# Zero fills of an attention and gated-product kernel: 64-KB pieces read from DRAM, and transfers of 3 MB

## The chip, the cores and the metric

The kernel runs on one core of one Trainium2 chip. The metric is device time in microseconds of one execution, lower is better. Times are given as the median of several runs; the profile is of one execution.

## What is computed

The program computes one decoding step of a transformer block and the gradients of everything in it. The block has an adaptive layer norm, attention over the last 4,096 positions of a cache, and a gated product:

```python
mod = (_silu(c) @ w_mod).reshape(c.shape[0], 6, 1, -1)
...
h = _layernorm(x, axis=-1) * (1 + ca) + sa
x = x + ga * _A_ref(h, A_k_cache, A_v_cache, A_wq, A_wo)
h = _layernorm(x, axis=-1) * (1 + cb) + sb
x = x + gb * _B_ref(h, B_w_gate, B_w_up, B_w_down)
return x
...
W = min(4096, max(256, Sk // 4))
k = jnp.repeat(k_cache[:, :, Sk - W:, :], rep, axis=1)
...
h = _sigmoid(g) * u
return jnp.einsum('bsf,fd->bsd', h, w_down)
```

There is one token (1,024 values), 32 query heads in 4 groups, head size 128, and a cache of 65,536 positions. The outputs are the result and its gradients for x, both caches, wq, wo, w_gate, w_up, w_down, c and w_mod, in bf16. The gradients of the two caches (out_2 and out_3) have the shape of the whole cache, and only the last 4,096 of 65,536 positions of a group are used. The other 61,440 rows of each of the 8 groups are zero and still must be written: 15.7 MB a group, 125.8 MB in all, two thirds of what the kernel writes. These writes are the zero fills.

## The kernel before

The work is written in one order by hand (the program is not rescheduled), and each engine's instructions run in that order. DMA transfers are issued on two queues. POOL issues most of them, the zero fills among them. SP issues the loads of w_down and the stores of its gradient, and some stores at the very end.

The stages, with the times of the profile: loads of keys, values and wq with the first products (to some 70 us); a first long product stage, keys times weighted values, at L646 to L679 (73 to 155 us); a second long product stage, the function `bch` at L702 (155 to about 285 us); a stretch that forms the combined weights (to some 310 us); the gated product at L1047 to L1092, seven rounds over blocks of 512 columns (to some 476 us); and a closing stage that writes the remaining gradients.

The zero fills are cut into 120 units of about 1 MB (P x ZW bf16 values, ZW = 4096) in the list `zleft` (L142 to L149). Of these, 15 units are columns of group 0 of out_2, and each of the other seven groups gives 15 contiguous units. Seven units of group 0 are "narrow" (at the places in NARROW, L38): they leave out 8 of 128 rows, which are written elsewhere.

The function `zero(n, after, big)` at L164 takes the next n units off the list and issues them on POOL. `after` makes the issue wait for a matmul, which paces the fills. A fill is written in one of three ways:

- from the tile `zeros` in SBUF, 128 rows of 8 KB (L186). The tile holds FP8 zeros, and the transfer widens them to FP32, so that it reads a quarter of what it writes;
- with `big`, from DRAM to DRAM, declared as 32 rows of 32 KB (L180). It reads zeros from `zero_src`, a unit that was filled first, again as FP8;
- narrow, also from SBUF (L173 and L176).

`big` is given in the two long product stages alone (L660 and L714). How many units are taken at each place stands in the lists Z_GA to Z_END (L48 to L57): four before the attention scores are done (L495), four at L543, 31 in the first long stage (Z_N, one at about each fourth step), 42 in the second (Z_B) with four more beside it, 5 in the stretch after it (Z_FOLD), 27 in the gated product (Z_FFN) and 3 in the closing stage.

In a round of the gated product, w_down comes in two halves of 512 KB on SP (`load_wd`, L872). PE multiplies with a half (L999), DVE forms its sums (L227) and overwrites it in place with its gradient (L223), and SP stores it (`store_wd`, L875); the next round's half is loaded into the same place when that store has landed. The blocks of w_up and w_gate are loaded by POOL (L886), used by PE (L981), overwritten by DVE and ACT, and stored by POOL (L890), in two buffers that alternate between rounds.

Of the kernel before, what the change touches and what calls it, by code (L numbers as in the profile page):

```python
# [10 lines left out]
P = 128  # L11
FP32 = mybir.dt.float32
BF16 = mybir.dt.bfloat16
FP8 = mybir.dt.float8e4
# [11 lines left out]
G = 4  # L26
# [11 lines left out]
NARROW = (15, 45, 75, 93, 103, 113, 119)  # L38

def spread(total, n):
    return [(i + 1) * total // n - i * total // n for i in range(n)]

NBP = 8
NT = 8
NGA = 9
# [5 lines left out]
Z_N = spread(31, 128)  # L53
Z_B = [n + (i in (31, 38)) for i, n in enumerate(spread(29, 43))] + [1, 1, 1, 1, 0] + [1, 0, 0, 1, 1, 1, 0, 0] + [1, 0, 1, 0, 1, 0, 0, 0]
# [4 lines left out]
def kernel(  # L59
# [26 lines left out]
    nc = tc.nc  # L86
    SKW = A_k_cache.shape[2] - W
# [16 lines left out]
    def vt(shape, name, dt=FP32):  # L104
        return pool.tile(shape, dt, name=name)
# [4 lines left out]
    ZW = 4096  # L110
    zeros = vt([P, ZW // 2], "zeros", FP8)
# [11 lines left out]
    def fill_rows(og, g):  # L123
        return og[0, g, 0:SKW, :].rearrange("r d -> (r d)")

    first_rows = fill_rows(out_2, 0).rearrange("(p x) -> p x", p=P)
    NZR = first_rows.shape[1] // ZW
    zregions = [first_rows[:, i * ZW:(i + 1) * ZW] for i in range(NZR)]
    flat = []
    for og in (out_2, out_3):  # L130
        for g in range(G):
            if og is not out_2 or g:
                whole = fill_rows(og, g).rearrange("(i x) -> i x", i=NZR)
                flat.extend(whole[i:i + 1, :] for i in range(NZR))

    zero_src = flat.pop(0)
    BIGP = 32

    def as_rows(piece, n):
        return piece.rearrange("i (p x) -> (i p) x", p=n)  # L140

    wide = [as_rows(zero_src, P)] + zregions[len(NARROW):] + flat  # L142
    narrow = zregions[0:len(NARROW)]
    zleft = []
    while narrow or wide:
        if narrow and (len(zleft) in NARROW or not wide):
            zleft.append((narrow.pop(0), True))
        else:
            zleft.append((wide.pop(0), False))  # L149
    nlen = len(NARROW)  # L150
    ncount = list(range(1, nlen + 1))
    NS = SKIP + 1
    rest = out_2[0, 0, 0:SKW, :].rearrange("r d -> (r d)").rearrange("(p x) -> p x", p=P)[0:8, 0:nlen * ZW].bitcast(FP32)
    assert nlen * 2 <= 20

    keep = [0]

    def dep(later, earlier):
        tc.add_manual_dep(later.ins, earlier.ins.name,
# [1 line left out]
                          reason="pace")  # L161

    def zero(n, after=None, big=False):  # L164
        for _ in range(n):
            if len(zleft) <= keep[0]:
                return
            region, narrow_ = zleft.pop(0)
            first = None
            if narrow_:  # L170
                nc.gpsimd.inc_swdge_sem([], [], mode="reset_dge_cursor")
                n = nlen - ncount.pop()
                first = nc.gpsimd.dma_start(  # L173
                    out=rest[0:NS, 0:nlen * 128].rearrange("p (t x) -> p t x", t=2)[:, :, n * 64:(n + 1) * 64],
                    in_=zeros[0:NS, 0:64].rearrange("p (t x) -> p t x", t=1).broadcast_to([NS, 2, 64]))
                ins = nc.gpsimd.dma_start(  # L176
                    out=region[8:P, :].bitcast(FP32).rearrange("(t p) x -> p t x", t=2),
                    in_=zeros[0:60, :].rearrange("p (t x) -> p t x", t=1).broadcast_to([60, 2, ZW // 2]))
            elif big and region.shape[0] == 1:
                ins = nc.gpsimd.dma_start(  # L180
                    out=as_rows(region, BIGP).bitcast(FP32),
                    in_=zero_src[:, 0:P * ZW // 4].rearrange("i (p x) -> (i p) x", p=BIGP).bitcast(FP8))
            else:
                if region.shape[0] == 1:
                    region = as_rows(region, P)
                ins = nc.gpsimd.dma_start(out=region.bitcast(FP32), in_=zeros[:, :])  # L186
            if after is not None:
                dep(first or ins, after)

# [19 lines left out]
    def tt(out, a, b, op):  # L209
        return nc.vector.tensor_tensor(out=out, in0=a, in1=b, op=op)  # L210
# [215 lines left out]
    for j in range(KD):  # L426
        for k in range(16):
            mm = nc.tensor.matmul(mod_ps[:, k:k + 1], lhsT=wm01_t[j][:, k * P:(k + 1) * P],
                                  rhs=cs_bf[:, j:j + 1], start=(j == 0 and k == 0), stop=(j == KD - 1),
                                  skip_group_check=True)  # L430
# [53 lines left out]
    for j in range(KD):  # L484
# [6 lines left out]
        for h in range(HQ):  # L491
            mm = nc.tensor.matmul(q_ps[:, h:h + 1], lhsT=wq_t[j][:, h * P:(h + 1) * P],  # L492
                                  rhs=h1_bf[:, j:j + 1], start=(j == 0 and h == 0), stop=(j == KD - 1),
                                  skip_group_check=True)
# [9 lines left out]
    for ch in range(8):  # L504
        ps = new_ps("sc_ps")
        for g in range(G):
            mm = nc.tensor.matmul(ps[32 * g:32 * g + 32, 0:512], lhsT=q_col2[:, HG * g:HG * g + 32],
                                  rhs=k_T[:, g, ch * 512:(ch + 1) * 512], start=True, stop=True,
                                  tile_position=(0, 32 * g))
# [132 lines left out]
    def recent(mm, lag):  # L642
        last_mm.append(mm)
        return last_mm[-lag] if len(last_mm) >= lag else last_mm[0]

    for g in range(G):  # L646
        nbank = bank_pair("n_ps", g)
        for t_ in range(KT):
            s = g * KT + t_
            vp = vp_t[(s // 2) % 2]  # L650
            if t_ % 2 == 0:
                tt(vp.rearrange("p t h d -> p (t h d)"),
                   v_nat[:, g, t_ * DH:(t_ + 2) * DH].rearrange("p (t o d) -> p t o d", t=2, o=1).broadcast_to([P, 2, HG, DH]),
                   pT2[:, g, HG * t_:HG * t_ + 2 * HG, :].rearrange("p n (o k) -> p n o k", o=1).broadcast_to([P, 2 * HG, 64, 2]),
                   ALU.mult)
            for k in range(2):
                mm = nc.tensor.matmul(nbank[k][:, :], lhsT=k_nat[:, g, t_ * DH:(t_ + 1) * DH],  # L657
                                      rhs=vp[:, t_ % 2, 4 * k:4 * k + 4, :].rearrange("p h d -> p (h d)"),
                                      start=(t_ == 0), stop=False)
            zero(Z_N[s], recent(mm, 6), True)  # L660
            if t_ == 20:
                build_bd(g)
            if s == 2:
                ok_cols(ok4)
            elif s == 4:
                ok_rows()
            elif s == 24:
                mod_gb((6, 7))
                load_wo(0)
            elif t_ % 2 == 1:  # L670
                side()
        for k in range(2):
            nc.tensor.matmul(nbank[k][:, :], lhsT=nkb_rows[:, :], rhs=bd[:, 4 * k:4 * k + 4, :].rearrange("p h d -> p (h d)"),
                             start=False, stop=True)
            c0 = (HG * g + 4 * k) * P
            nc.scalar.activation(out=N_sb[:, c0:c0 + 512], in_=nbank[k][:, :], func=ACT.Copy, scale=float(SCALE))
        load_wo(4 + g)
        if g < 3:
            jobs.extend(t_unit(h, "AA") for h in range(HG * g, HG * g + HG))  # L679
# [5 lines left out]
    bq = []  # L685
# [13 lines left out]
    nbq = len(bq)  # L699
    bbank = {}  # L700

    def bch(n=1):  # L702
        for _ in range(n):
            if not bq:
                return
            p, i, u = bq.pop(0)
            if i == 0:
                bbank[p] = bank_pair("b_ps", p)
            for a in range(4):
                h = 4 * u + a  # L710
                for k in range(2):
                    mm = nc.tensor.matmul(bbank[p][k][:, :], lhsT=a4[:, p, h, :], rhs=wo_t[u][:, a, k * 512:(k + 1) * 512],  # L712
                                          start=(i == 0 and a == 0), stop=(i == 7 and a == 3))
            zero(Z_B[nbq - 1 - len(bq)], recent(mm, 3), True)  # L714
            if i == 7:
                for k in range(2):
                    o = B_t[p][:, k * 512:(k + 1) * 512]
                    if k == 0 or p == NBP - 1:
                        nc.scalar.copy(out=o, in_=bbank[p][k][:, :])
                    else:  # L720
                        cp(o, bbank[p][k][:, :])
# [418 lines left out]
    dh1_ps = new_acc("dh1_ps")  # L1140
    for p in range(NBP):
        for it in range(KD):
# [95 lines left out]
    dh1 = vt([P, KD], "dh1")  # L1238
    cp(dh1[:, 0:NBP], dh1_ps[:, 0:NBP])
    dwo(4)  # L1240
# [34 lines left out]
    dx0b, _ = layernorm_bwd_col(dln1, ln1, rstd1, "ln1b")  # L1275
# [58 lines left out]
    for g in (2, 3):  # L1334
# [1 line left out]
        dwq_tile(4 + g, tail)  # L1336
        s2(2 * g, tail)
        s2(2 * g + 1, tail)
    keep[0] = 0
    zero(len(zleft))  # L1340
    assert not zleft and not narrow and not jobs and not bq

# [28 lines left out]
```

## Time and profile before

| | |
|---|---|
| median of 3 runs | 595.29 us (595.26 to 595.35) |
| the profiled execution | 595.61 us |
| its span, first to last instruction | 593.8 us |
| busy share of the span | PE 68%, DVE 60%, ACT 44%, POOL 26% |
| moved by DMA | 246.61 MB, mean 415 GB/s |
| HBM | 78.39 MB read, 185.60 MB written |
| fills from SBUF (zeros, 1,024 KB each) | 44, median 13.7 us from issue to landing |
| fills from DRAM | 69, median 16.9 us from issue to landing |
| narrow fills (960 KB each) | 7, median 14.5 us from issue to landing |

How to read the lines that follow. A line of a busy table gives a stretch in us from the span's start, its length, the busy time of PE, PE's weight loads, DVE, ACT and POOL with their instructions, the granted clock of PE, the mean busy share of the 16 DMA engines (packets overlap, so it can pass 1) and GB/s. A line of the chain of waits gives a start, a duration and what ran; "DMA a<-b" is a transfer from b to a from its issue to its landing. A line of the timeline gives a start, a busy time, the engine, the line of the program, and in brackets how long the engine was idle before and what ended that. Of the queues, q0 is the one that POOL issues on and q1 that of SP, each with packets, MB and its share of the 16 engines' time. "POOLq" and "SPq" are those engines' issuing sides. The trace also has a record of each DMA packet (start, duration, size, queue) and the 16 times at which the DMA engines report that their share of a transfer has landed.

### The profile page before, as it was taken

Reading aid. Unit: us, or ns where it says so; the run is one execution under the profiler, and the core shown is the slowest. Engines: PE = TensorE matmul, PEld = TensorE weight load, DVE = VectorE, ACT = ScalarE, POOL = GpSimd, SP = SyncE. Lnnn points to the kernel's source line nnn. Section 1 sums busy time; section 2 is a strip of 40 time slices with the busy share of each in tenths; the row PEclk is TensorE's granted clock in tenths of the full one; section 3 lists DMA queues with packets and bytes.
Section 4 is the critical chain, followed back from the end, with each engine's and each line's share of the span. In section 5 each row is a group of like instructions: output and inputs, shape, how many; then the busy total and the mean of one; then the engine's idle time right before and its main releaser. Section 6 shows DMA issues by size and latency. Waiting matters only on the chain.

```text
span 593.8 us, 10908 instructions
## 1 busy us (share of the span) xinstructions
PE 406.3 (68%) x4516; PEld 271.3 (46%) x4516; DVE 356.7 (60%) x674; ACT 263.6 (44%) x401; POOL 156.2 (26%) x255
## 2 busy tenths in 40 slices
PE   3997789999999989998876236344455294894410
PEld 3995434334344545544445225334344264593410
DVE  3754499999511010086628686596877885868650
ACT  2489514557211014213125366463665833893310
POOL 3113113212222112222221333223334252222200
PEclk9999699999999999999985566565555576855555
DMA  9999999999999999999999999999999999999997
GB/s 351 421 416 422 412 461 393 448 429 427 426 421 403 442 446 411 443 425 402 412 418 402 418 413 414 411 409 405 398 392 418 420 417 426 418 423 426 425 421 328
DMA packets 36321, 246.61 MB, mean 415 GB/s; under 512 B 5141, under 2 KB 5141, under 8 KB 22552
## 3 DMA queue, kind: packets, MB, share of 16 engines
q0 software_dynamic: 28976, 218.64, 91.8%
q1 hardware_dynamic: 7248, 27.27, 12.9%
q8 instruction: 35, 0.57, 0.4%
q14 instruction: 14, 0.11, 0.0%
q10 hardware_dynamic: 48, 0.01, 0.0%
HBM read 78.39 MB, written 185.60 MB: 445 GB/s over the span
## 4 chain that ended last, share of the span: by engine, by line
DMA 47%; PE 19%; DVE 17%; issue 6%; ACT 5%; POOL 1%; ACTq 0%; DVEq 0%; POOLq 0%; SPq 0%
DMA out_dram<-arena 16%; DMA out_dram<-out_dram 16%; PE n_ps L657 6%; DMA arena<-in_B_w_gate_dram 6%; DVE arena L227 5%; DVE arena L223 5%; DVE arena L210 4%; DMA arena<-in_B_w_down_dram 3%; DMA out_dram<-zeros 3%; DMA arena<-in_w_mod_dram 3%; ACT arena L476 2%; PE t_ps L619 2%; PE w_ps L415 1%; PE tp_k L455 1%; PE b_ps L712 1%
## 5 line engine op out<-in xcount | busy, mean ns | idle before, releaser
L712 PE MATMUL b_ps<-arena 128*128 128x512 bf16 x512 | 115.9, 379 | 1.1 <-ACT arena L858 1.1
L858 ACT COPY arena<-tp_side 128x1024 bf16<-128x1024 bf16 x62 | 60.9, 1014 | 70.3 <-PE tp_side L857 68.6
L210 DVE TENSOR_TENSOR arena<-arena 128x2048 bf16<-128x2048 bf16 x64 | 76.6, 1223 | 2.3 <-PE n_ps L657 0.3
L712 PEld LDWEIGHTS <-arena 128*128 128x128 bf16 x512 | 48.7, 98 | 57.6 <-issue 2.9
L227 DVE CUSTOM_DVE_ANT_0 arena<-arena,scr 128x1024 bf16<-128x1024 bf16 x56 | 66.3, 1222 | 9.8 <-ACT scr L1020 9.8
L657 PE MATMUL n_ps<-arena 128*128 128x512 bf16 x256 | 65.8, 378 | 6.2 <-DVE arena L210 4.6
L180 POOL DMA_DIRECT2D out_dram<-out_dram x69 | 34.1, 495 | 118.6 <-PE n_ps L657 36.0
L857 PE MATMUL tp_side<-ident_bf,arena 128*128 128x128 bf16 x496 | 55.5, 290 | 9.7 <-ACT arena L858 5.0
L857 PEld LDWEIGHTS <-arena 128*128 128x128 bf16 x496 | 47.3, 135 | 15.4 <-issue 8.5
L981 PE MATMUL fg<-h_bf,arena 128*128 128x1 bf16 x448 | 15.6, 166 | 44.3 <-DMA arena<-in_B_w_up_dram 26.2
L657 PEld LDWEIGHTS <-arena 128*128 128x128 bf16 x256 | 24.6, 97 | 41.6 <-issue 16.2
L227 DVE CUSTOM_DVE_ANT_0 arena<-arena,b1k 128x1024 bf16<-128x1024 bf16 x24 | 28.4, 1221 | 19.5 <-PE fg L999 19.5
L186 POOL DMA_DIRECT2D out_dram<-zeros x44 | 24.8, 565 | 56.8 <-PE q_ps L492 16.1
L258 ACT ACTIVATE arena<-scr,h 128x1024 bf16<-128x1024 bf16 x35 | 38.5, 1142 | 2.3 <-DVE dh2acc L227 1.8
L890 POOL DMA_DIRECT2D out_dram<-arena x28 | 22.1, 795 | 65.8 <-ACT arena L258 46.5
L1200 ACT ACTIVATE arena<-ps_kv 128x512 bf16<-128x512 f32 x48 | 26.2, 687 | 23.1 <-PE ps_kv L1196 22.9
L621 ACT CAST arena<-t_ps 128x512 bf16<-128x512 f32 x56 | 30.1, 589 | 12.1 <-PE t_ps L619 12.1
L981 PEld LDWEIGHTS <-arena 128*128 128x128 bf16 x448 | 13.9, 105 | 46.9 <-DMA arena<-in_B_w_up_dram 27.7
L219 DVE CAST arena<-b_ps 128x512 bf16<-128x512 f32 x6 | 4.2, 692 | 51.1 <-PE b_ps L712 51.1
L1196 PE MATMUL ps_kv<-junk,arena 8*128 8x128 bf16 x256 | 27.3, 305 | 8.7 <-DVE arena L223 7.6
L1196 PEld LDWEIGHTS <-arena 8*128 8x128 bf16 x256 | 25.3, 141 | 10.5 <-issue 10.5
L476 ACT COPY arena<-tp_wq 128x1024 bf16<-128x1024 bf16 x23 | 21.7, 1044 | 7.8 <-PE tp_wq L474 7.7
(310 smaller groups left out, 648.1 us busy)
## 6 DMA issues: line engine op xcount, KB each, us to landing
out_dram<-zeros POOLq DMA_DIRECT2D x44, 1024.0 KB, 13.7
out_dram<-arena POOLq DMA_DIRECT2D x28, 1024.0 KB, 17.4
out_dram<-arena POOLq DMA_DIRECT2D x30, 512.0 KB, 11.0
out_dram<-arena SPq DMA_DIRECT2D x20, 512.0 KB, 9.8
arena<-in_A_wq_dram POOLq DMA_DIRECT2D x8, 1024.0 KB, 20.6
arena<-in_A_wo_dram POOLq DMA_DIRECT2D x8, 1024.0 KB, 13.2
arena<-in_w_mod_dram POOLq DMA_DIRECT2D x7, 1024.0 KB, 18.0
arena<-in_B_w_up_dram POOLq DMA_DIRECT2D x14, 512.0 KB, 11.6
```

The lines of the kernel that those rows point to most:

```text
L180: ins = nc.gpsimd.dma_start(out=as_rows(region, BIGP).bitcast(FP32), in_=zero_src[:, 0:P * ZW // 4].rearrange("i (p x) -> (i p) x", p=BIGP ...
L210: return nc.vector.tensor_tensor(out=out, in0=a, in1=b, op=op)
L223: return nc.vector.tensor_scalar(out=out, in0=a, scalar1=s1, scalar2=None, op0=op0)
L227: return nc.vector.tensor_tensor_reduce(out=out, in0=w, in1=b, scale=1.0, scalar=0.0, op0=ALU.mult, op1=ALU.add, accum_out=acc)
L258: return nc.scalar.activation(out=out, in_=b, func=ACT.Copy, scale=col)
L476: nc.scalar.copy(out=blk, in_=tp[:, :])
L621: nc.scalar.copy(out=o, in_=ps)
L657: mm = nc.tensor.matmul(nbank[k][:, :], lhsT=k_nat[:, g, t_ * DH:(t_ + 1) * DH], rhs=vp[:, t_ % 2, 4 * k:4 * k + 4, :].rearrange("p h d -> ...
L712: mm = nc.tensor.matmul(bbank[p][k][:, :], lhsT=a4[:, p, h, :], rhs=wo_t[u][:, a, k * 512:(k + 1) * 512], start=(i == 0 and a == 0), stop= ...
L857: nc.tensor.transpose(tp[:, i * P:(i + 1) * P], blk[:, i * P:(i + 1) * P], ident_bf[:, :])
L858: nc.scalar.copy(out=blk if dst is None else dst, in_=tp[:, :])
L1196: nc.tensor.matmul(ps[:, t4 * DH:(t4 + 1) * DH], lhsT=rows[32 * g:32 * g + HG, t_ * P:(t_ + 1) * P], rhs=hd[32 * g:32 * g + HG, :], start= ...
```

## The change

The list of fills is built anew, and `zero` counts credits. The first eight units are still written from SBUF. All others except the narrow ones are written from DRAM to DRAM in rows of 64 KB, 16 rows for a unit. Four of the seven whole groups (TRIPLE) are cut into 5 pieces of 3 MB instead of 15 of 1 MB. Such a piece is taken once there are three credits, from the ninth unit on, where no narrow unit falls between; the 20 pieces of 3 MB all lie in the two long product stages. The last eight units of group 0 are now 16 rows each by 64 KB, not 128 rows by 8 KB, and come at the end of the list. The counts in the lists Z_Q to Z_END, the places of the narrow units and every other transfer stay.

```diff
+NCHIP = 8
+TRIPLE = (1, 3, 3, 3, 3, 1, 1)
...
+    for i, (og, g) in enumerate([(out_2, 1), (out_2, 2), (out_2, 3), (out_3, 0), (out_3, 1), (out_3, 2), (out_3, 3)]):
+        mine = fill_rows(og, g).rearrange("(i x) -> i x", i=NZR // TRIPLE[i])
+        (single if TRIPLE[i] == 1 else triple).extend(mine[k:k + 1, :] for k in range(mine.shape[0]))
+    zero_src = single[0]
+    single.extend(first_rows[16 * k:16 * k + 16, nlen * ZW:] for k in range(8))
+
     zleft = []
-    while narrow or wide:
-        if narrow and (len(zleft) in NARROW or not wide):
-            zleft.append((narrow.pop(0), True))
+    at = 0
+    while narrow or single or triple:
+        if narrow and at in NARROW:
+            zleft.append((narrow.pop(0), "narrow", 1))
+        elif triple and at >= NCHIP and at + 3 <= next(i for i in NARROW if i >= at):
+            zleft.append((triple.pop(0), "long", 3))
         else:
-            zleft.append((wide.pop(0), False))
-    nlen = len(NARROW)
+            zleft.append((single.pop(0), "chip" if at < NCHIP else "long", 1))
+        at += zleft[-1][2]
...
-    def zero(n, after=None, big=False):
-        for _ in range(n):
-            if len(zleft) <= keep[0]:
-                return
-            region, narrow_ = zleft.pop(0)
+    def zero(n, after=None):
+        credit[0] += n
+        while zleft and credit[0] >= zleft[0][2]:
+            region, kind, size = zleft.pop(0)
+            credit[0] -= size
...
-            elif big and region.shape[0] == 1:
+            elif kind == "chip":
+                ins = nc.gpsimd.dma_start(out=region.rearrange("i (p x) -> (i p) x", p=P).bitcast(FP32), in_=zeros[:, :])
+            else:
+                rows = 16 * size
+                if region.shape[0] == 1:
+                    region = region.rearrange("i (p x) -> (i p) x", p=rows)
                 ins = nc.gpsimd.dma_start(
-                    out=as_rows(region, BIGP).bitcast(FP32),
-                    in_=zero_src[:, 0:P * ZW // 4].rearrange("i (p x) -> (i p) x", p=BIGP).bitcast(FP8))
-            else:
-                if region.shape[0] == 1:
-                    region = as_rows(region, P)
-                ins = nc.gpsimd.dma_start(out=region.bitcast(FP32), in_=zeros[:, :])
+                    out=region.bitcast(FP32),
+                    in_=zero_src[:, 0:rows * 8192].rearrange("i (p x) -> (i p) x", p=rows).bitcast(FP8))
...
-            zero(Z_N[s], recent(mm, 6), True)
+            zero(Z_N[s], recent(mm, 6))
...
-            zero(Z_B[nbq - 1 - len(bq)], recent(mm, 3), True)
+            zero(Z_B[nbq - 1 - len(bq)], recent(mm, 3))
```

More of the change, by code (lines that the diff above doesn't have):

```diff
@@ L126 @@
     first_rows = fill_rows(out_2, 0).rearrange("(p x) -> p x", p=P)
+    nlen = len(NARROW)
     NZR = first_rows.shape[1] // ZW
[L128 to L143, printed above, removed]
-    zleft = []
-    while narrow or wide:
-        if narrow and (len(zleft) in NARROW or not wide):
-            zleft.append((narrow.pop(0), True))
-        else:
-            zleft.append((wide.pop(0), False))
-    nlen = len(NARROW)
+    assert NZR - nlen == 8 and NZR % 3 == 0
+    narrow = [first_rows[:, i * ZW:(i + 1) * ZW] for i in range(nlen)]
+    single = []
+    triple = []
+    for i, (og, g) in enumerate([(out_2, 1), (out_2, 2), (out_2, 3), (out_3, 0), (out_3, 1), (out_3, 2), (out_3, 3)]):
[3 more added lines that the diff above has]
+    single.extend(first_rows[16 * k:16 * k + 16, nlen * ZW:] for k in range(8))
+    zleft = []
+    at = 0
[4 more added lines that the diff above has]
+            zleft.append((triple.pop(0), "long", 3))
+        else:
+            zleft.append((single.pop(0), "chip" if at < NCHIP else "long", 1))
+        at += zleft[-1][2]
+    assert not narrow and not triple and at == NZR * 8
     ncount = list(range(1, nlen + 1))
     NS = SKIP + 1
-    rest = out_2[0, 0, 0:SKW, :].rearrange("r d -> (r d)").rearrange("(p x) -> p x", p=P)[0:8, 0:nlen * ZW].bitcast(FP32)
+    rest = first_rows[0:8, 0:nlen * ZW].bitcast(FP32)
     assert nlen * 2 <= 20
-    keep = [0]
+    credit = [0]
     def dep(later, earlier):
@@ L161, in dep @@
                           reason="pace")
-    def zero(n, after=None, big=False):
-        for _ in range(n):
-            if len(zleft) <= keep[0]:
-                return
-            region, narrow_ = zleft.pop(0)
+    def zero(n, after=None):
[3 more added lines that the diff above has]
+            credit[0] -= size
             first = None
-            if narrow_:
+            if kind == "narrow":
                 nc.gpsimd.inc_swdge_sem([], [], mode="reset_dge_cursor")
@@ L1338 @@
         s2(2 * g + 1, tail)
-    keep[0] = 0
-    zero(len(zleft))
+    zero(sum(size for _, _, size in zleft))
     assert not zleft and not narrow and not jobs and not bq
```

## The prediction

> **What bounds the kernel now.** I read the page's slices first, then its queues and issues, then busy time by stretch, the chain of waits, and last the single lines.
>
> ```profile
> DMA  9999999999999999999999999999999999999997
> q0 software_dynamic: 28976, 218.64, 91.8%
> q1 hardware_dynamic: 7248, 27.27, 12.9%
> out_dram<-zeros POOLq DMA_DIRECT2D x44, 1024.0 KB, 13.7
> out_dram<-out_dram POOLq DMA_DIRECT2D x69, 16.9
> ```
>
> The DMA engines are full in 39 of 40 slices. 246.61 MB in 593.8 us are 415 GB/s, and no compute engine is above 68% busy. The trace's packet records say the same: between 3.1 and 588.9 us the only gaps of some size are at 412.5 and 441.7 us (1.7 and 1.0 us, summed over 16 DMA engines). So an edit counts in two ways only: it changes how long the DMA engines need for the same bytes, or it lets them run dry. q0 is POOL's queue with nearly all bytes. q1, SP's, carries w_down in and out in the gated product.
>
> ```profile
> 70.00:155.00 85.00, 77.82 (x391) 32.98 (x384) 77.86 (x79) 40.22 (x95) 19.41 (x37) 0.99 1.06 432
> 200.00:285.00 85.00, 79.36 (x670) 43.29 (x669) 27.52 (x63) 19.00 (x24) 19.70 (x35) 1.00 1.03 424
> 390.00:476.00 86.00, 36.17 (x530) 31.94 (x530) 67.29 (x147) 52.99 (x58) 29.11 (x43) 0.52 1.11 407
> ```
>
> Last column: 432 and 424 GB/s in the two product stages, 407 in the gated product. PE is nearly full in the first two, so there the fills only ride along. In the gated product PE and DVE wait for DMA, in a loop:
>
> ```profile
> 315.72 10.62 DMA out_dram<-arena
> 326.42 9.20 DMA arena<-in_B_w_down_dram
> ...
> 342.86 9.35 DMA out_dram<-arena
> 352.27 10.19 DMA arena<-in_B_w_down_dram
> ```
>
> This is SP's leg twice over: the gradient of w_down leaves a buffer, and only then can the next block be loaded there. From 380 us on the chain runs through POOL's stores and loads of w_gate instead.
>
> **Part 1: packet size in the product stages.** Nothing changes here. The packet records hold 1,104 packets of 65,536 bytes, which is 69 x 16: the DRAM fills, declared as 32 rows of 32 KB, already go out as one 64-KB packet to each of the 16 DMA engines. Cost 0.
>
> **Part 2: 36 fills from SBUF become fills from DRAM.** 44 issues have zeros as source and 1,024 KB; eight remain. By the landing records the four SBUF fills issued at 66.1 to 67.7 us land at 74.37, 76.83, 79.23 and 81.67: 2.43 us each. DRAM fills issued from 198.8 us land at 217.91, 220.34, 222.74, 225.16 and 227.57: 2.415 us each. So 36 x 0.018 = 0.65 us are saved. The far end is the last SBUF fills, which land at 489.63, 492.07, 494.53 and 496.98 (2.45): 36 x 0.035 = 1.3 us. The other end is 0. I take -0.7, since the 66-us row is the one without other traffic.
>
> **Part 3: three fills in one transfer.** 60 fills become 20 issues, so POOL is spared 40 x 0.495 = 20 us. POOL is 26% busy and waits for PE or for landings before fills, so that is 0 on the path. A fill's 64-KB packet takes 2.431 us and fills land every 2.415, so nothing is left between transfers to save. The far end is the 4-byte completion packet that follows a DRAM fill, 52 ns: 40 x 0.052 = 2.1 us saved. I take 0, by the landings. Only eight POOL transfers are in flight at once (the ninth, at 15.15 us, follows the first one's landing at 14.87). In triples, eight hold more bytes; but POOL's order stays, the engines stay full, and a load behind the same bytes lands at the same time.
>
> The Trainium skill (DMA: Bandwidth & Descriptors, "Anatomy of one DMA") gives each such transfer about 2 us that do not grow with its size, and its rules for authors advise merging. Paid in full, 40 fewer would save an estimated 80 us. The trace disagrees: queued fills land 2.415 us apart, less than the packet itself takes.
>
> **Part 4: the first triple is late.** A triple needs three credits. The third of the first long stage is the line at 79.97:
>
> ```profile
> 74.11 0.53 POOL L186 DMA_DIRECT2D out_dram<-zeros  x1 [5.88 <-PE n_ps L657]
> 76.21 0.52 POOL L180 DMA_DIRECT2D out_dram<-out_dram  x1 [1.56 <-PE n_ps L657]
> 79.97 0.50 POOL L180 DMA_DIRECT2D out_dram<-out_dram  x1 [3.24 <-PE n_ps L657]
> ```
>
> Afterwards the first two issue nothing. Of the fills before them the last lands on the first DMA engine at 79.73 and on the last at 81.67. From issue to first packet I take 2.3 us (the load at 440.26, where engines were idle until 442.59). So data starts at 82.3, and engines idle 2.6 us (first) to 0.6 us (last). I take 0.6, since the end belongs to the engines that are behind; ends 0 and 2.6. The next triple is issued 7.0 us later (the line at 86.98), less than the 7.25 us of three fills, so no second gap.
>
> **Part 5: SP behind 64-KB packets.** In the gated product a fill has been eight 8-KB packets to each DMA engine (322 ns at the median); now it is one of 2,431 ns. The nearest row is the same load at two times. At 283 and 296 us 64-KB fills were in flight beside POOL loads; later there were only 8-KB fills:
>
> ```profile
> L872 SPq DMA_DIRECT2D arena<-in_B_w_down_dram x2: 328/328/328, 283.3 to 296.5; - x2
> DMA to landing us min/median/max: 13.2/13.2/13.2
> ...
> L872 SPq DMA_DIRECT2D arena<-in_B_w_down_dram x12: 339/340/340, 326.4 to 447.4; - x12
> DMA to landing us min/median/max: 9.0/9.7/10.4
> ```
>
> 13.2 against 9.7 is 3.5 us for a leg of SP. Of the four legs in the chain above, the first three run while wide fills land (those issued at 309.7 to 320.0, 333.4, 334.0 and 343.3); the fourth meets the tail of one and a narrow one, which keeps its packets. That is 3 x 3.5 = 10.5 us later in computing. DMA engines idle only for what their queue does not cover: when POOL issues the next stores, at 351.39, its last queued fill has 5.8 us to go on the median DMA engine (357.20); less 2.3 us to start, 3.5 us are covered. So +7.0. In the later five rounds the chain is POOL's and SP has slack: a w_down block that landed at 429.95 is stored from 435.86, 5.9 us later, against some 3.6 us of work (409.02 to 412.64), so 2.3 us; another (434.7 to 439.21) has about 0.9. I take 0 there. Ends of part 5: 0 (SP's legs shrink as the queue empties, POOL's get shorter) and 7.0 + 5 x 1.5 = 14.5 us.
>
> The Trainium skill (DMA: Bandwidth & Descriptors, "Queues, rings and completion order") says that a DMA engine takes turns between queues and drains a whole packet first. By that rule a leg waits for about one wide packet: 3 x 2.43 - 3.5 = 3.8 us in place of 7.0, and the forecast would be 598.7. The row of 13.2 agrees in sign and says more.
>
> **Sum.** -0.7 + 0 + 0.6 + 7.0 = +6.9 us. The profiled execution has a span of 593.8 and took 595.61 us, 1.8 around it; that is 0.32 over the median of 595.29. 595.61 + 6.9 = 602.5, and against the median 602.2.
>
> **Rivals.**
>
> 1. *Faster, 593.5.* SP's legs stay covered and parts 2 and 3 pay at their far ends, counted half for the second: -1.3 - 1.05 + 0.6 = -1.75, so 593.5; without the late start 592.9. For it: DMA is the bound everywhere, so every ns per packet counts, and POOL writes 36 small-packet fills less. Against: the landings give 0.018 us a fill. Chance 0.27.
> 2. *The same, 595.2.* Parts 2 and 4 cancel (-0.7 + 0.6) and the queue covers part 5. For it: from 380 us the chain is POOL's. Against: four SP legs on the chain at 315 to 362 us. Chance 0.20.
> 3. *Slower (the forecast)*: one mechanism, SP's packets behind 64-KB packets at 315 to 360 us; it decides as soon as the lateness is over the 3.5 us covered, which is one leg at the price of 3.5. Its own range is 597 to 610. Chance 0.53. Were SP behind in every later round as well, it would be 595.3 - 0.1 + 14.5 = 609.7.
>
> That part of the change does nothing is sure: the packet size in the product stages.
>
> **Numbers.** Forecast 602.2. What a measurement here can tell from no change is about 0.2%, 1.2 us. Faster 0.27, within 0.20, slower 0.53. The range goes from 593.0 (the faster rival, short of its last end) to 610.0, the upper end of part 5; about 0.15 is left out, on both sides together.
>
> **What would show it.** In the new profile: 8 issues from zeros of 1,024 KB, 20 of 3 MB; packet records only of 64 KB in the product stages (part 1); fills landing 2.41 us apart in the gated product (2); triples landing 7.25 us apart (3); a gap of DMA near 80 to 82 us (4); SP's w_down loads near 13 us to landing, an 8 in the DMA line between 315 and 480 us, and a later start of the closing stage, now 476 us (5). I am wrong if SP's legs stay near 10 us, or lengthen while the DMA line stays at 9: then the queue covers more than 3.5 us, or the legs were not what held the loop.

## The result, and the profile after

The changed kernel is **slower by 0.37%**: 597.80 us (median of 20 runs, 596.03 to 600.08) against 595.62 (20 runs, 595.26 to 596.55), ratio 1.0037, interval 1.0030 to 1.0044. The profiled execution has a span of 596.5 us, 2.7 over that of before. The forecast was slower, 602.2.

The page after: the DMA line, the queues, and from its list of transfers those of SP's stores of 512 KB and of the fills from SBUF; below them SP's stores before.

```profile
DMA  8999999999999999999999999999999999999998
q0 software_dynamic: 24304, 218.64, 89.6%
q1 hardware_dynamic: 7248, 27.27, 11.6%
...
out_dram<-arena SPq DMA_DIRECT2D x20, 512.0 KB, 13.6
out_dram<-zeros POOLq DMA_DIRECT2D x8, 1024.0 KB, 8.7
```

```profile
out_dram<-arena SPq DMA_DIRECT2D x20, 512.0 KB, 9.8
```

On POOL's queue the same bytes go out in 4,672 packets fewer, and SP's stores of 512 KB take 13.6 us to landing where the median was 9.8. The slices of the DMA line are too coarse to show where the time went. Two short stretches do, first before, then after (last two columns: busy share and GB/s):

```profile
79.50:82.50 3.00, 2.59 (x11) 0.96 (x10) 3.00 (x4) 0.90 (x4) 0.69 (x2) 1.00 1.34 513
356.00:364.00 8.00, 5.63 (x105) 5.39 (x102) 4.18 (x10) 3.18 (x5) 2.54 (x5) 0.50 1.15 416
```

```profile
79.50:82.50 3.00, 2.44 (x10) 0.96 (x10) 3.00 (x4) 2.02 (x7) 0.53 (x1) 1.00 0.87 341
356.00:364.00 8.00, 3.39 (x43) 2.90 (x41) 7.69 (x18) 7.23 (x10) 1.71 (x2) 0.50 0.90 311
```

GB/s of a stretch this short depends on which packets start in it; the drop is what counts. By the packet records, DMA engines stand still for 1.77 us on the mean of the 16 at 79.4 to 82.7, and for 0.96 us in two gaps at 357.9 to 369.9. All such idle time between 3.1 and 588.9 us comes to 2.74 us; before it was 0.24. The difference, 2.5 us, is nearly the growth of the span, 2.7. So it looks as if the change costs time by letting the DMA engines run dry in two places; the next lines say how, and the experiments test it. POOL's issues at the start of the first long stage, after:

```profile
67.62 1.61 POOL L181 DMA_DIRECT2D out_dram<-zeros  x3
81.09 0.53 POOL L186 DMA_DIRECT2D out_dram<-out_dram  x1 [11.86 <-PE n_ps L659]
88.11 0.53 POOL L186 DMA_DIRECT2D out_dram<-out_dram  x1 [6.48 <-PE n_ps L659]
```

POOL waits 11.86 us for the third credit. The last fill before it lands at 79.84 on the first DMA engine and at 81.66 on the last. And the chain of waits at the start of the gated product, after:

```profile
317.37 15.02 DMA out_dram<-arena
...
332.46 7.34 DMA arena<-in_B_w_down_dram
...
340.22 9.70 DMA arena<-in_B_w_gate_dram
...
350.88 10.19 DMA out_dram<-arena
...
361.13 5.61 DMA arena<-in_B_w_down_dram
```

The first store takes 15.02 us (10.62 before), but the loads behind it take 7.34 and 5.61 (9.20 and 10.19 before). Which transfer ended a wait is inferred by the view, and for the load of w_gate the timeline does not bear it out: PE waits until 347.01 us for the second half of w_down, and DVE then works from 347.41 to the store at 350.88 without a pause over 0.1 us. So the way to that store leads through the second half. Its store and load are not in this chain; the part on the prediction gives their times.

### The profile page after: what moved, and what is told of

Same layout as the page of the kernel before. It is cut to its first block, busy times and chain, and to the rows that moved or that the text cites. A ratio compares the mean times of both kernels' runs of the same rounds, so it can differ in the third digit from the quotient of the medians.

```text
span 596.5 us, 10813 instructions
## 1 busy us (share of the span) xinstructions
PE 402.6 (67%) x4492; PEld 268.2 (45%) x4516; DVE 356.8 (60%) x674; ACT 263.4 (44%) x401; POOL 136.1 (23%) x215
## 4 chain that ended last, share of the span: by engine, by line
DMA 38%; PE 22%; DVE 17%; issue 14%; ACT 3%; POOL 1%; ACTq 0%; DVEq 0%; POOLq 0%; SPq 0%
DMA out_dram<-arena 16%; DMA out_dram<-out_dram 7%; PE n_ps L659 6%; DMA arena<-in_B_w_gate_dram 6%; DMA arena<-in_B_w_down_dram 6%; DVE arena L225 5%; DVE arena L229 5%; DVE arena L212 4%; DMA arena<-in_w_mod_dram 3%; PE b_ps L714 3%; PE t_ps L621 2%; PE tp_wq L476 2%; PE w_ps L417 2%; PE tp_k L457 1%; ACT arena L478 1%
## 5 line engine op out<-in xcount | busy, mean ns | idle before, releaser
L714 PE MATMUL b_ps<-arena 128*128 128x512 bf16 x495 | 113.8, 379 | 2.1 <-ACT arena L860 1.1
L859 PE MATMUL tp_side<-ident_bf,arena 128*128 128x128 bf16 x496 | 54.2, 284 | 10.0 <-ACT arena L860 5.2
L1001 PE MATMUL fg<-hh_bf,arena 128*128 128x1 bf16 x224 | 7.9, 166 | 29.8 <-DMA arena<-in_B_w_down_dram 27.3
## 6 DMA issues: line engine op xcount, KB each, us to landing
out_dram<-arena SPq DMA_DIRECT2D x20, 512.0 KB, 13.6
```

Source lines behind the costliest of these rows:

```text
L859: nc.tensor.transpose(tp[:, i * P:(i + 1) * P], blk[:, i * P:(i + 1) * P], ident_bf[:, :])
```

## The experiments

All were timed beside the kernel before, in three groups of four (e1 to e4; e5 to e8; e9 to e12); its median was 595.58, 595.56 and 595.54. The theories: **A**, the late first piece of 3 MB; **B**, SP's transfers behind 64-KB packets in the gated product, which the prediction held to be nearly all; **C**, DRAM fills or 3-MB pieces cost the DMA engines time as such. Each had 11 runs (e7 12, e8 4).

| run | us | ratio to before, 95% |
|---|---|---|
| e1_first_triple_later | 596.55 | 1.0018 (1.0010 to 1.0027) |
| e2_sbuf_in_gated | 596.81 | 1.0017 (1.0008 to 1.0026) |
| e3_both_undone | 595.58 | 0.9997 (0.9989 to 1.0006) |
| e4_before_all_wide | 596.47 | 1.0016 (1.0007 to 1.0025) |
| e5_paid_after | 595.09 | 0.9991 (0.9983 to 1.0000) |
| e6_wide_85_92 | 596.62 | 1.0016 (1.0007 to 1.0024) |
| e7_wide_from_94 | 595.03 | 0.9995 (0.9985 to 1.0006) |
| e8_dram_8k | 607.09 | 1.0190 (1.0177 to 1.0203) |
| e9_dram_8k_spread | 596.12 | 1.0008 (0.9999 to 1.0016) |
| e10_combined | 594.56 | 0.9984 (0.9975 to 0.9993) |
| e11_wide_85_89 | 595.83 | 1.0008 (0.9999 to 1.0017) |
| e12_wide_90_92 | 595.37 | 0.9998 (0.9989 to 1.0007) |

### Undoing one part, the other, and both

**e1**, no 3-MB piece before place 16:

```diff
-        elif triple and at >= NCHIP and at + 3 <= next(i for i in NARROW if i >= at):
+        elif triple and at >= 16 and at + 3 <= next(i for i in NARROW if i >= at):
```

> The changed kernel, but no piece of 3 MB before the 17th unit (place 16), so that the first long stage starts with single fills as before. In the changed kernel's profile the DMA engines idle 1.77 us each, on the mean, at 79.4 to 82.7 us, and 0.96 us at 357.9 to 369.9. Theory A (the late first piece of 3 MB is most of the loss): no gap at 80 us, and 1.7 us less, about 596.1. Theory B (SP's transfers behind 64-KB packets in the gated product are most of it): 597.5, the gap at 358 us stays or grows. Theory C (64-KB fills or 3-MB pieces take the DMA engines longer as such): 597.8, no change beyond noise.

**e2**, from place 85 on from SBUF:

```diff
-    single.extend(first_rows[16 * k:16 * k + 16, nlen * ZW:] for k in range(8))
+    single.extend(first_rows[:, (nlen + k) * ZW:(nlen + k + 1) * ZW] for k in range(8))
...
-            zleft.append((single.pop(0), "chip" if at < NCHIP else "long", 1))
+            zleft.append((single.pop(0), "chip" if at < NCHIP or at >= 85 else "long", 1))
...
```

> The changed kernel, but from place 85 on (after the second long stage) all units are written from SBUF in 8-KB pieces as before, and the last eight units of group 0 are columns again. The pieces of 3 MB stay as they are. Theory A: the gap at 80 us stays, only the 0.8 us at 358 us go: 597.0. Theory B: SP's w_down transfers are back at 9 to 10 us and the time is near that of before, 595.8. Theory C: 596.5 if it is the DRAM fills, 597.8 if it is the 3-MB pieces.

**e3**, both edits:

> Both edits of the two kernels above together: no piece of 3 MB before place 16, and 8-KB pieces from SBUF from place 85 on. Theories A and B: both gaps gone, 595.3 (within 0.5 of the kernel before). Theory C with the pieces of 3 MB as the cause: 597 or more.

**e4**, the kernel before with wide packets (64 KB, from DRAM) for all its contiguous units from the first long stage on, and no 3-MB pieces:

```diff
-    def zero(n, after=None, big=False):
+    def zero(n, after=None, big=True):
```

> The kernel before, with one edit: all its contiguous units are written from DRAM in 64-KB packets, in the gated product and the closing stage too. No pieces of 3 MB. Theory A: no gap at 80 us, a gap of some 0.8 us near 360 us: 596.1. Theory B: 597.5. Theory C with DRAM fills as the cause: 597.8.

Both theories hold, with about half each. Taking the first cause away saves 597.80 - 596.55 = 1.25 us, and with the second one already gone 596.81 - 595.58 = 1.23. Taking the second away saves 0.99 (597.80 - 596.81) or 0.97 (596.55 - 595.58). e4, the second alone, is 0.89 slower than before. Each of these differences is uncertain by some 0.5 us, so that they agree this closely is in part luck. With both gone nothing is left (e3), though it still writes 20 pieces of 3 MB, so C is out for these to within the interval of some 0.5 us; for DRAM fills e7 below answers. The profiles agree. e1 has no gap at 80 us and 0.9 us at 355.9 to 362.4; e2 has 2.2 us at 79.5 to 83.1 and none at 358; e3 has neither.

### Is it the piece, or its lateness?

**e5**, e2 with every 3-MB piece issued at its first credit and the two others paid afterwards:

```diff
-        while zleft and credit[0] >= zleft[0][2]:
+        while zleft and credit[0] >= 1:
```

> The changed kernel with 8-KB pieces from SBUF from place 85 on, and one edit more: a piece of 3 MB is issued at its first credit instead of its third, and the two others are paid afterwards. The pieces stay where they are, the first at places 8 to 10. Without that edit the kernel took 596.81, and DMA stood still for 2.2 us at 80 us. If the late issue is the cause of that part: no gap at 80 us and 595.5, as with both parts undone (595.58). If pieces of 3 MB cost something as such there: 596.8.

595.09, 1.7 less than e2. The first piece goes out at 72.44 us, and the gap is gone:

```profile
72.44 0.53 POOL L188 DMA_DIRECT2D out_dram<-out_dram  x1 [3.79 <-PE n_ps L661]
80.64 0.53 POOL L188 DMA_DIRECT2D out_dram<-out_dram  x1 [7.66 <-PE n_ps L661]
```

The same piece at the same place in the list leaves no gap when it is paid for afterwards, so it is its lateness that cost the 1.2 us. The other 0.5 us (e5 is that much below e3) is not explained: the edit also issues the 19 other pieces earlier, and DMA idle time in e5 is no less than before.

### Which units hold SP up

**e6**, **e11** and **e12** give wide packets to a few units of the kernel before, **e7** to all from place 94 on:

```diff
-            elif big and region.shape[0] == 1:
+            elif (big or 85 <= 119 - len(zleft) <= 92) and region.shape[0] == 1:
```

(85 to 89 in e11, 90 to 92 in e12, `94 <= 119 - len(zleft)` in e7.)

> The kernel before, with 64-KB packets from DRAM for the units of places 85 to 92 alone (issued at about 300 to 343 us: the run of five ahead of the gated product and the first three in it); all later ones from SBUF as before. If the loss is the lateness of the first two rounds, where four SP transfers stand in the chain of waits: gap near 358 us as with all units wide, and 596.3 to 596.5. If the loss is spread over all rounds: 595.8.

> The complement: the kernel before, with 64-KB packets from DRAM for the units from place 94 on alone (from about 357 us), the earlier ones after the second long stage from SBUF. If the loss is in the first two rounds: no gap near 358 us and 595.6. If it is spread over all rounds: 596.3. If the source in DRAM or the packet size costs the DMA engines time as such: 596.2 (25 of 35 units).

> The kernel before, with 64-KB packets for places 85 to 89 alone (the five units ahead of the gated product; four of them stand behind one another when the first gradient of w_down is stored). If the first store, late behind that run, starts the loss: 596.4, most of the 1.06 us of places 85 to 92 together. If the later units count as much: 596.0.

> The complement: 64-KB packets for places 90 to 92 alone (the first three units in the gated product). If the first store starts the loss: 595.5. If all legs of the first two rounds count alike: 596.0.

Eight units cost all of it: e6 is 1.06 over before, and the 23 later ones (e7; three of its 26 places are narrow, and the expectation's 25 is a miscount) cost nothing, at 0.53 below before within an interval that holds 1. In e11, with five wide units, the first stores already take 14.9 us. SP's two first stores, before and then in e11:

```profile
L875 SPq DMA_DIRECT2D out_dram<-arena x2: 343/346/348, 315.7 to 319.2; - x2
...
DMA to landing us min/median/max: 10.6/10.6/10.6
```

```profile
L875 SPq DMA_DIRECT2D out_dram<-arena x2: 343/346/348, 315.9 to 319.4; - x2
...
DMA to landing us min/median/max: 14.9/14.9/14.9
```

e11 also has the gap (0.81 us at 356.7 to 362.1), and POOL's first store of the next round goes out at 357.6 instead of 351.4. Yet its time is only 0.29 over before. e12 has no gap there but one of 0.45 us at 384.0 to 387.9, and is 0.17 under. The two do not add up to 1.06. With intervals of some 0.5 us to each side, whether the late start needs both groups to cost 1 us stays open.

### Packet size or source

**e8** and **e9** keep DRAM as the source but write 8-KB packets, in the kernel before, for all contiguous units from place 85 on (the five ahead of the gated product, those in it and in the closing stage) and for four in the second long stage that were written from SBUF. In e8 all rows read the same 2 KB, in e9 each row its own:

```diff
-                if region.shape[0] == 1:
+                dram = region.shape[0] == 1
+                if dram:
...
-                ins = nc.gpsimd.dma_start(out=region.bitcast(FP32), in_=zeros[:, :])
+                ins = nc.gpsimd.dma_start(
+                    out=region.bitcast(FP32),
+                    in_=as_rows(zero_src, P)[:, 0:ZW // 4].bitcast(FP8) if dram else zeros[:, :])
```

That is e9; in e8 the source is `zero_src[:, 0:ZW // 4].bitcast(FP8).broadcast_to([P, ZW // 2])`.

> The kernel before, with the source of the fills from the gated product on in DRAM, but in 8-KB packets (each row reads the same 2 KB of zeros). If the packet size is what holds SP's transfers up: SP's stores of the gradient of w_down at 9 to 10 us to landing, no gap near 358 us, 595.6. If it is the source in DRAM: stores near 13.5 us as with wide fills, 596.4.

> As the run with 8-KB packets from DRAM, but each row reads 2 KB of its own, 8 KB apart, not all the same 2 KB. That run took 607.09, with 361 GB/s at 465 to 500 us against 421 before, so it told nothing of SP's transfers. If many reads of one place were its cost: 595.6 here, w_down stores at 9 to 10 us, no gap near 358 us (then it is the packet size that holds SP up). If small reads from DRAM cost as such: 600 or more. If the source in DRAM is what holds SP up: stores near 13.5 us and 596.4.

e8 told nothing of SP: it slowed everything (see the last section). In e9 SP's stores are as before:

```profile
DMA to landing us min/median/max: 7.6/10.0/11.1
```

10.0 at the median (before 9.8; after 13.6 in the line below), no gap near 358 us, and POOL's store of the second round at 351.5 (before 351.4). So it is the packet's size that holds SP up and opens the gap, not its source.

```profile
DMA to landing us min/median/max: 8.2/13.6/15.0
```

e9's time is 0.58 over before, with an interval that just holds 1. If that is real, it is not idle time of the DMA engines (0.21 us in all, before 0.24); what it is stays open. So e9 shows what the packets do to SP and to the gap, and not that 8-KB packets from DRAM are as fast as those from SBUF.

### A version faster than both

**e10** keeps the change without its two losses:

```diff
-        while zleft and credit[0] >= zleft[0][2]:
+        while zleft and credit[0] >= 1:
...
-            zleft.append((single.pop(0), "chip" if at < NCHIP else "long", 1))
+            zleft.append((single.pop(0), "chip" if at < NCHIP or 85 <= at <= 92 else "long", 1))
```

> The changed kernel with both losses taken out and the rest kept: a piece of 3 MB is issued at its first credit, and the units of places 85 to 92 are written from SBUF in 8-KB pieces; wide packets from place 94 on. The two gains seen alone (595.09 against 595.58, and 595.03 against 595.56) add up to 594.5 if they are of the DMA engines' own time; 595.0 if they are one and the same.

594.56, 0.98 below before (ratio 0.9984, interval 0.9975 to 0.9993) and 3.2 below the changed kernel. Its largest gap inside the run is 0.06 us, at 438 us. That the two gains add up is what the medians say; neither is resolved alone.

## Why the prediction was wrong

The sign was right, and so were the two places where the DMA engines run dry. The sum of +6.9 us was three times the measured +2.2, because part 5 went wrong. Step by step:

- **Part 1** (no cost): right. There are 1,680 packets of 65,536 bytes after, 16 for each of the 105 DRAM units, and none longer. A 3-MB piece is 48 such packets.
- **Part 2** (-0.7): neither contradicted nor shown. e7 does it for 23 units and is 0.5 lower, within its interval of no change. But e4 does it for 27 units that e6 leaves in SBUF, and the two are only 0.15 apart.
- **Part 3** (0): 3-MB pieces that follow one another land 7.28 us apart (after: 133.90 and 141.18 us), three times 2.43. e3 has them and is level with before. The far end, 2.1 us saved, is out.
- **Part 4** (+0.6): the gap was forecast in its place and measured 1.77 us, and it costs 1.2. Three things were mis-sized. I took over the 79.97 us of before as the time of the third credit; it was 81.09 in this execution, and 81.50 in e2, as PE began the stage at 74.3 and 74.7 rather than 73.2. In the fourteen profiles it begins between 71.5 and 75.1, and only the two kernels with the late piece have a gap there. The start took less than the 2.3 us assumed: the DMA engines begin the piece 1.2 to 1.6 us after POOL begins to issue it (82.32 to 82.69). And all DMA engines wait, not the slowest alone. After the gap they are level: the piece lands between 90.12 and 90.68, where the fill before it had landed between 79.84 and 81.66. If part of the idle time only takes away the lead of some engines, that would explain why 1.8 to 2.2 us of it cost 1.2; it was not tested.
- **Part 5** (+7.0): this is the step that failed, measured at 1.0 us. It added up three legs of SP and compared them with what the queue covers when POOL issues its next store. But only two legs stand ahead of that store, and the queue covered more.

The lines of part 5, first before, then after: PE's wait for the second half of w_down, and POOL's next store.

```profile
338.86 0.59 PE L999 MATMUL fg<-hh_bf,arena 128*128 128x1 bf16 x16 [2.61 <-DMA arena<-in_B_w_down_dram]
351.39 1.71 POOL L890 DMA_DIRECT2D out_dram<-arena  x2 [5.95 <-ACT arena L258]
```

```profile
347.01 0.58 PE L1001 MATMUL fg<-hh_bf,arena 128*128 128x1 bf16 x16 [6.57 <-DMA arena<-in_B_w_down_dram]
359.54 1.71 POOL L892 DMA_DIRECT2D out_dram<-arena  x2 [12.69 <-ACT arena L260]
```

Both moved by 8.15 us, so POOL's store follows the second half of w_down. By the landing records its store and load took 15.0 and 11.1 us, against 10.9 and 8.7: 4.1 + 2.4 = 6.5 us, and the other 1.65 had come from the gap at 80 us (the first store starts at 317.37 instead of 315.72). The third leg that I priced, the store at 342.86 before, landed at 352.21, when POOL's store had gone out; it could not make that store later. So POOL was 6.5 us late, not 10.5; two legs at the forecast's own price would have given 7.0 - 3.5 = +3.5. Nor did the queue cover 3.5 us only: 6.5 us late left 0.96 us idle. SP's own late transfers, 1.0 MB between 356 and 362 us, gave the DMA engines work while POOL had none. Then the lateness paid itself back in part. With nothing queued before it, the fourth leg took 5.61 us instead of 10.19, which I had named as the lower end and not used. By the fourth round POOL's first store is 3.6 us behind that of before, by the last 2.9, of which 1.65 are the early gap's. The prediction had named the sign of being wrong that came: legs grow longer while the DMA line stays at 9. Of SP's transfers the stores did (13.6 us against 9.8); the loads of w_down did not go to 13 us but from 9.8 to 9.2.

That the price of 3.5 us a leg lies near the mean of 4.1 and 2.4 is luck. The load from which it was read, 13.21 us at 296.54 before, took 9.22 us in the changed kernel, and between 8.9 and 13.6 us in the fourteen profiles.

The Trainium skill (DMA: Bandwidth & Descriptors, "Queues, rings and completion order") says that a DMA engine drains a whole packet of one queue before it switches to the next. A wait for one wide packet of 2.43 us fits the load, which was 2.4 us longer, but is too little for the two stores, which were 4.1 and 4.4 us longer. Of the 16 shares of the first store 12 land by 328.4, and four only at 331.9 to 332.4. The prediction's estimate by that rule comes to 599.0 (595.29 - 0.1 + 3.8; the 598.7 of the prediction is a slip). It was nearer than mine by luck too, as it adds up the same three legs.

The rivals: "faster" and "the same" both needed the queue to cover SP's legs. That nearly happened, with 0.96 of 6.5 us left over. A version with the two gaps closed is faster, as e10 shows, by 0.98 us and not the 1.8 of that rival.

## What to carry to other kernels

Where transfers fill the DMA engines, a late transfer costs only what the queue ahead of it does not hold, so look for the thin places of the queue: here a piece three times as large, issued at its last credit, came late by two credits and cost 1.2 us, and issued at the first it left no gap. A run of long packets on one queue delayed the transfers of another queue that shares the DMA engines (15.0 us against 10.6); keep packets short where another queue's round trip is on the chain. Later in the same loop long ones cost nothing that was measured (e7). When lateness goes round a loop, do not add up its legs: ask for each leg which later issue really waits for it, and remember that a queue that runs short can make the next leg faster (5.6 us against 10.2).

## What the runs showed that was not expected

Reading the same 2 KB of DRAM for every row of a fill was dear here. At 465 to 500 us, where fills are most of the traffic, e8 and then e9 (the same packets, each row reading its own 2 KB):

```profile
465.00:500.00 35.00, 20.58 (x358) 17.12 (x359) 27.52 (x80) 22.87 (x29) 10.93 (x15) 0.65 1.17 361
```

```profile
465.00:500.00 35.00, 19.41 (x354) 15.71 (x354) 24.39 (x73) 19.66 (x25) 12.91 (x18) 0.65 1.15 416
```

361 against 416 GB/s, and 607.09 (four runs) against 596.12 us in all, for a source that differs in nothing else. The wide fills read places of their own within one transfer, and land 2.415 us apart for 1 MB in the profile before.

Idle time of the DMA engines accounts for the losses only roughly. Against before, by one profile each, idle time and span grew by 2.5 and 2.7 us in the changed kernel, 0.9 and 0.8 in e1, 2.1 and 1.9 in e2, 0.7 and 0.5 in e4, 0.8 and 0.6 in e6, but 0.75 and 0.26 in e11. And in e5, e7 and e10 the span is 0.7 to 0.8 us shorter with about the same idle time as before, in e9 0.7 longer. What sets these apart is not shown.

The changed kernel also scatters more: 20 runs within 4.05 us, against 1.29 before. Neither loss alone does that: e2, with the late piece, has 1.55 us, and e1, with the other one, 1.72, while e3, with neither, has 0.61. But the runs of before beside them spread by 1.49 too, so what widens the changed kernel stays open.
